# Order and queues of the first transfers: the second half of row block 1, and the first half of Wv in two pieces

## The chip, the core and the metric

The kernel runs on one core of a Trainium2 chip. The core has five engines that run their own instruction streams: TensorE (PE; its weight loads are listed as PEld), VectorE (DVE), ScalarE (ACT), GpSimd (POOL) and SyncE (SP). Transfers between the chip's main memory and the on-chip memory are issued in this kernel from SP and from ACT, each in the order of its own stream, and are carried out by 16 DMA engines that serve both queues (q1 in the profile holds SP's transfers, q10 ACT's). The metric is the device time of one execution in microseconds (us), as the median over runs. The profile is of one further execution; its span runs from the first to the last profiled instruction.

## What is computed

Input x has 2048 rows of 640 values in bf16. It is normalised by rows, and the normalised rows feed two branches: an attention with 32 heads of 20 values, worked in four segments of 512 rows with a running memory between them, and a gated feed-forward branch of width 1536.

```python
xn = _layernorm(x, axis=-1)                       # (x - mean) / sqrt(var + 1e-5)
s = _A_ref(xn, A_wq, A_wk, A_wv, A_wo, A_beta)     # q, k, v = xn @ wq, wk, wv; 4 segments; @ wo
g = _silu(_B_ref(xn, B_w_gate, B_w_up, B_w_down))  # (sigmoid(xn@wg) * (xn@wu)) @ wd
return x + s * g
```

For this change only the beginning matters: x of the first segment and the weights wv, wk, wq come in, the rows are normalised and transposed, and v, then k, then q of the first segment are computed.

## The kernel before

**Tiles.** A segment n is 512 rows, held as four row blocks j of 128 rows (128 partitions) by 640 columns in the tile `xt4` (in the profile `xt`). Each row block has two halves of HD = 320 columns. Weights lie as five chunks (DC = 5) of 128 input rows; `Wv` is 128 partitions x 5 chunks x 640 columns and is loaded in two column halves of 320, `load_wv(0, ...)` and `load_wv(1, ...)` (L149 to L151). A half of `Wv` is 400 KB, a half of a row block 80 KB.

**Order.** The kernel is scheduled by hand: on each engine and queue the instructions run in the order in which the program issues them, and waits between engines come from semaphores that the framework sets by tile and part of a tile. A transfer counts a completion semaphore up to 16. There are eight of these for the transfers of both queues, used in turn, and a transfer waits until the one that last used its semaphore has landed.

**First transfers** (L154 to L164), in program order. On SP: block 0 first half, block 1 first half, block 1 second half, block 2 whole, `Wv` second half, `Wk`, `Wq`, beta. On ACT: block 0 second half, `Wv` first half, block 3 whole; then an activation (L169) that loads the table for square roots, and much later, behind `root0(1)` and `root0(2)`, the weights `Wg` and `Wu`.

**Normalising segment 0** (L648 to L720). For each row block j:

- `half_stats0(j, i)` (L651, VectorE): statistics of half i of the block; it needs that half of x.
- `moments0(j)` (L654, VectorE): mean and variance from the two halves' statistics.
- `root0(j)` (L657, ScalarE): square root of the variance.
- `norm0(j)` (L662, L665, VectorE): reciprocal, then the normalised rows `xn`, for block 0 in two pieces of columns.
- `transpose0(j)` (L675, TensorE): five transposes of 128x128 into `pT`; chunks 0 to 2 are copied into `xnT` by ScalarE (L680), chunks 3 and 4 by VectorE (L678).
- `do_V(0, j, half)` (L344): five matmuls `psv` over the chunks k with `xnT` and `Wv`, evacuated by ScalarE.

On VectorE the order around the change is: statistics of block 0, moments 0, statistics (1, 0), norm 0, statistics (1, 1), moments 1, statistics (2, 0), copy of `xnT` of block 0, norm 1, statistics (2, 1), statistics (3, 0), moments 2, and so on. On TensorE `keep_warm` matmuls into `wps`, whose result nobody uses, stand between the first pieces of real work. After the last `do_V` TensorE goes on with `do_K` and `do_Q` of segment 0 (`psq`, L281), then with gate and up products, attention and the other segments in one fixed order.

Of the kernel before, what the change touches and what calls it, by code (L numbers as in the profile page):

```python
# [9 lines left out]
P = 128  # L10
D = 640
# [6 lines left out]
DC = D // P  # L18
# [4 lines left out]
HD = D // 2  # L23
# [52 lines left out]
def kernel(  # L76
# [14 lines left out]
    nc = tc.nc  # L91
# [36 lines left out]
    def load_x(n, a=0, b=4, cols=slice(0, D), eng=nc.sync):  # L128
        if n not in xt_of:
            xt_of[n] = lnp.tile([P, 4, D], BF, name="xt4", bufs=3)  # L130
        src = x2[n * L:(n + 1) * L, :].rearrange("(j p) d -> p j d", p=P)
        eng.dma_start(xt_of[n][:, a:b, cols], src[:, a:b, cols])
# [6 lines left out]
    Wv = cpool.tile([P, DC, D], BF, name="Wv")  # L139
# [6 lines left out]
    nc.vector.memset(warm[:, 0:L], 0.0)  # L146
    beta_b = cpool.tile([P, H], BF, name="beta_b")

    def load_wv(half, eng):  # L149
        hs = slice(half * HD, (half + 1) * HD)  # L150
        eng.dma_start(Wv[:, :, hs], A_wv[:, hs].rearrange("(c p) n -> p c n", p=P))  # L151


    load_x(0, 0, 1, slice(0, HD))  # L154
    load_x(0, 0, 1, slice(HD, D), nc.scalar)
    load_x(0, 1, 2, slice(0, HD))
    load_wv(0, nc.scalar)
    load_x(0, 1, 2, slice(HD, D))
    load_x(0, 2, 3)
    load_x(0, 3, 4, eng=nc.scalar)  # L160
    load_wv(1, nc.sync)
    load_w(nc.sync, Wk, A_wk)
    load_w(nc.sync, Wq, A_wq)
# [626 lines left out]
    for p in range(0, OLD, 5):  # L790
        n, g = units[p][0], units[p][1][0][0]
# [216 lines left out]
```

## Time and profile before

| what | value |
|---|---|
| median of three timed runs | 317.45 us (317.26 to 317.47) |
| the profiled execution's own time | 317.27 us |
| its span | 315.6 us |
| granted TensorE clock, mean | 1.000 |
| busy, share of the span | PE 98%, PEld 53%, DVE 72%, ACT 72%, POOL 42% |

TensorE is busy almost throughout; VectorE and ScalarE have room on average. That average says little about the first 14 us, in which TensorE waits for rows to be normalised. TensorE's own work there, in order of time (start, length, engine, line, operation, tiles and shape):

```profile
5.20 0.55 PE L675 MATMUL pT<-ident,xn 128*128 128x128 bf16 x5
...
7.44 0.45 PE L675 MATMUL pT<-ident,xn 128*128 128x128 bf16 x5
...
9.35 0.45 PE L675 MATMUL pT<-ident,xn 128*128 128x128 bf16 x5
...
11.13 0.45 PE L675 MATMUL pT<-ident,xn 128*128 128x128 bf16 x5
11.42 2.20 PE L121 MATMUL psv<-Wv,xnT 128*128 128x320 bf16 x15
13.46 5.56 PE L121 MATMUL psq<-xnT,Wk 128*128 128x512 bf16 x25
```

The four rows of `pT` are the transposes of row blocks 0 to 3. [...] The queues' issues in the same view:

```profile
0.79 1.82 SPq L132 DMA_DIRECT2D xt<-in_A_x_dram  x4
2.65 0.43 SPq L151 DMA_DIRECT2D Wv<-in_A_wv_dram  x1
3.25 0.40 SPq L135 DMA_DIRECT2D Wk<-in_A_wk_dram  x1
3.70 0.52 SPq L135 DMA_DIRECT2D Wq<-in_A_wq_dram  x1
5.08 0.81 SPq L164 DMA_DIRECT2D beta_b<-in_A_beta_dram  x1
```

```profile
0.79 0.41 ACTq L132 DMA_DIRECT2D xt<-in_A_x_dram  x1
1.23 0.46 ACTq L151 DMA_DIRECT2D Wv<-in_A_wv_dram  x1
1.72 0.55 ACTq L132 DMA_DIRECT2D xt<-in_A_x_dram  x1
```

The length of such a row is the time in which the transfer is issued, not the time until its data are there. The row of four on SP holds the transfers of L154, L156, L158 and L159.

### The profile page before, as it was taken

To read this page: it belongs to the slowest core of one execution; us is meant where nothing else is said; L and a number is where in the kernel's file an instruction comes from. 1 tells how busy PE (TensorE), PEld (TensorE's weight loads), DVE (VectorE), ACT (ScalarE), POOL (GpSimd) and SP (SyncE) were. 2 spreads that over 40 slices of the span, in tenths; PEclk is the share of its full clock that TensorE was granted. 3 is DMA by queue.
4 is the path that set the end of the run, shared out by engine and by line. 5 is a ranking of instruction groups with operands and counts; after the bars stand their busy time and mean duration, and the time that the engine had idled before them with its cause. 6 is when DMAs were issued, how large, how long until landed. Compare 5 with 4: busy or idle time off the path is not lost.

```text
span 315.6 us, 10266 instructions
## 1 busy us (share of the span) xinstructions
PE 310.3 (98%) x4331; PEld 167.5 (53%) x4331; DVE 225.9 (72%) x512; ACT 227.2 (72%) x231; POOL 131.6 (42%) x227
## 2 busy tenths in 40 slices
PE   8999999999999999999999999999999999999995
PEld 4644445665545445654665454544466655444673
DVE  6473455765868988878869989788787776644575
ACT  3724478778798776778897869679897775777730
POOL 2580035535262534435453364444434353525313
PEclk9999999999999999999999999999999999999999
DMA  7984886420742364405953365139524000280202
GB/s 250 358 338 148 286 223 177 120 50 2 217 147 64 100 144 134 108 23 149 266 169 111 111 111 152 53 112 207 170 88 129 19 23 31 78 157 13 86 23 83
DMA packets 55390, 41.27 MB, mean 131 GB/s; under 512 B 25968, under 2 KB 53968, under 8 KB 55344
## 3 DMA queue, kind: packets, MB, share of 16 engines
q1 hardware_dynamic: 52800, 35.87, 41.1%
q10 hardware_dynamic: 2544, 4.75, 4.1%
q8 instruction: 34, 0.56, 0.8%
q14 instruction: 12, 0.10, 0.1%
HBM read 19.98 MB, written 14.73 MB: 110 GB/s over the span
## 4 chain that ended last, share of the span: by engine, by line
PE 96%; DMA 1%; DVE 1%; SPq 0%; issue 0%
PE up L121 12%; PE yp L121 11%; PE gp L121 11%; PE psq L121 10%; PE Sps L548 8%; PE gp L125 6%; PE yp L125 6%; PE up L125 6%; PE ApsT L572 6%; PE psv L121 5%; PE psq L125 4%; PE sp L121 3%; PE sp L125 3%; PE psv L125 2%; PE sp L532 2%; DMA xt<-in_A_x_dram 1%
## 5 line engine op out<-in xcount | busy, mean ns | idle before, releaser
L556 ACT ACTIVATE pt<-Sps 128x2048 bf16<-128x2048 f32 x80 | 150.3, 1878 | 40.8 <-PE Sps L548 39.5
L558 POOL TENSOR_SCALAR_AFFINE_SELECT pt<-pt 128x512 bf16<-128x512 bf16 x128 | 82.3, 658 | 156.0 <-ACT pt L556 153.2
L435 DVE SCALAR_TENSOR_TENSOR hT<-tg,up 128x512 bf16<-128x512 bf16 x48 | 32.6, 679 | 23.9 <-PE up L121 9.7
L121 PE MATMUL up<-xnT,Wu 128*128 128x512 bf16 x159 | 42.5, 380 | 0.0
L121 PE MATMUL gp<-xnT,Wg 128*128 128x512 bf16 x152 | 40.1, 380 | 0.0
L424 ACT ACTIVATE tg<-gp 128x512 bf16<-128x512 f32 x48 | 28.5, 595 | 14.4 <-PE gp L121 10.5
L121 PE MATMUL yp<-Wd,hT 128*128 128x320 bf16 x246 | 38.2, 300 | 0.0
L548 PE MATMUL Sps<-QT,KT 23*128 23x384 bf16 (+3 forms) x512 | 31.9, 301 | 0.0
L121 PEld LDWEIGHTS <-hT 128*128 128x128 bf16 x246 | 22.7, 98 | 11.3 <-issue 3.0
L580 DVE STREAM_TRANSPOSE tb<-ApsT 128x512 f32<-128x512 f32 x31 | 22.0, 711 | 4.2 <-PE ApsT L572 4.0
L452 DVE SCALAR_TENSOR_TENSOR aa<-t,yp 128x320 bf16<-128x320 bf16 x32 | 15.3, 478 | 13.5 <-ACT t L451 13.4
L125 PE MATMUL gp<-xnT,Wg 128*32 128x512 bf16 x352 | 24.4, 380 | 0.0
L572 PE MATMUL ApsT<-pt,V 128*32 128x512 bf16 (+2 forms) x496 | 23.5, 299 | 0.0
L121 PEld LDWEIGHTS <-Wu 128*128 128x128 bf16 x159 | 14.2, 98 | 17.4 <-issue 4.0
L121 PEld LDWEIGHTS <-Wg 128*128 128x128 bf16 x152 | 14.1, 98 | 15.8 <-issue 1.9
L125 PE MATMUL yp<-Wd,hT 128*32 128x320 bf16 x552 | 21.9, 300 | 0.0
L125 PE MATMUL up<-xnT,Wu 128*32 128x512 bf16 x324 | 21.7, 380 | 0.0
L548 PEld LDWEIGHTS <-KT 23*128 23x128 bf16 x512 | 9.1, 92 | 23.4 <-issue 23.4
L592 DVE STREAM_TRANSPOSE obT<-ob 128x256 f32<-128x256 f32 x31 | 13.5, 434 | 11.1 <-POOL ob L589 11.0
L589 POOL TENSOR_TENSOR ob<-tb,rb 128x320 bf16<-128x320 f32 x27 | 19.9, 736 | 2.3
L121 PE MATMUL psq<-xnT,Wq 128*128 128x512 bf16 x85 | 19.5, 379 | 0.0
L572 PEld LDWEIGHTS <-V 128*32 128x32 bf16 x496 | 14.4, 97 | 8.1 <-ACT tg L424 0.2
(124 smaller groups left out, 448.3 us busy)
## 6 DMA issues: line engine op xcount, KB each, us to landing
KT<-Kd SPq DMA_DIRECT2D x32, 80.0 KB
QT<-Qd SPq DMA_DIRECT2D x32, 80.0 KB
out_dram<-xt SPq DMA_DIRECT2D x14, 160.0 KB
Wg<-in_B_w_gate_dram ACTq DMA_DIRECT2D x1, 1920.0 KB
Wu<-in_B_w_up_dram ACTq DMA_DIRECT2D x1, 1920.0 KB
xt<-in_A_x_dram SPq DMA_DIRECT2D x3, 640.0 KB
Wd<-in_B_w_down_dram SPq DMA_DIRECT2D x1, 1920.0 KB
Od<-odot SPq DMA_DIRECT2D x3, 640.0 KB
```

The source lines that it names most:

```text
L121: nc.tensor.matmul(out_, lhsT=lhsT, rhs=rhs, start=start, stop=stop, skip_group_check=True)
L125: nc.tensor.matmul(out_[cols], lhsT=lhsT[:, cols], rhs=rhs, start=start, stop=stop, tile_position=(0, 32 * r), skip_group_check=True)
L424: nc.scalar.activation(tg[:], gp[:], ACT.Tanh, scale=0.5)
L435: nc.vector.scalar_tensor_tensor(out=h[:], in0=seg[n]["tg"][:], scalar=1.0, in1=up[:], op0=ALU.add, op1=ALU.mult)
L452: nc.vector.scalar_tensor_tensor(out=s["aa"][j][:, hs], in0=t2[:], scalar=1.0, in1=yp[:], op0=ALU.add, op1=ALU.mult)
L548: nc.tensor.matmul(Sps[:, r, c0:c0 + ncol], lhsT=KT[32 * r:32 * r + DH + 3, g, kb * P:(kb + 1) * P], rhs=QT[32 * r:32 * r + DH + 3, g, q0: ...
L556: nc.scalar.activation(pt[:, :, 0:ntot], Sps[:, :, 0:ntot], ACT.Exp, scale=SCALE)
L558: nc.gpsimd.affine_select(out=pt[:, :, c0:c0 + P], in_=pt[:, :, c0:c0 + P], compare_op=ALU.is_ge, fill=0.0, base=0, pattern=[[0, 4], [1, P ...
L572: nc.tensor.matmul(ps[32 * r:32 * r + 32, q0:L], lhsT=Vflat[n % 2][:, off:off + 32], rhs=t[:, r, c0:c0 + ncol], start=(i == 0), stop=(i == ...
L580: nc.vector.transpose(tb[:].rearrange("p h e -> p (h e)"), ps[:].rearrange("p (a t b) -> p a b t", t=32, b=2))
L589: eng.tensor_tensor(to, of, by, op=ALU.mult)
L592: nc.vector.transpose(s["obT", g // 4][:, g % 4, :].bitcast(F32), ob[:].rearrange("p a e b -> p (a e b)").bitcast(F32))
```

## The change

The second half of row block 1 moves from SP's queue to ACT's and stands there ahead of `Wv`, as the second transfer. The first half of `Wv`, one transfer on ACT before, becomes two: chunks 0 to 2 on ACT, chunks 3 and 4 on SP, where they take the place that the second half of block 1 had. All else stays as it was. SP's issues ahead of `Wk` stay five in number; ACT's ahead of the table load go from three to four.

```diff
-    def load_wv(half, eng):
+    def load_wv(half, eng, c0=0, c1=DC):
         hs = slice(half * HD, (half + 1) * HD)
-        eng.dma_start(Wv[:, :, hs], A_wv[:, hs].rearrange("(c p) n -> p c n", p=P))
+        eng.dma_start(Wv[:, c0:c1, hs], A_wv[c0 * P:c1 * P, hs].rearrange("(c p) n -> p c n", p=P))
 
 
     load_x(0, 0, 1, slice(0, HD))
     load_x(0, 0, 1, slice(HD, D), nc.scalar)
     load_x(0, 1, 2, slice(0, HD))
-    load_wv(0, nc.scalar)
-    load_x(0, 1, 2, slice(HD, D))
+    load_x(0, 1, 2, slice(HD, D), nc.scalar)
+    load_wv(0, nc.scalar, 0, 3)
+    load_wv(0, nc.sync, 3, DC)
     load_x(0, 2, 3)
     load_x(0, 3, 4, eng=nc.scalar)
     load_wv(1, nc.sync)
```

## The prediction

> **What bounds the kernel now.** I began with the page's chain of work that ended last. By engine it is
>
> ```profile
> PE 96%; DMA 1%; DVE 1%; SPq 0%; issue 0%
> ```
>
> TensorE holds the whole span except for a small share of DMA and VectorE. The change touches only the first transfers, so the next view is that chain in order of time, over its first 60 us (start, length, what):
>
> ```profile
> 1.66 0.05 issue
> 1.71 3.82 DMA xt<-in_A_x_dram
> 5.53 0.02 issue
> 5.55 0.50 DVE st L651
> ...
> 6.29 0.36 DVE st L651
> 6.64 0.20 DVE xnT L678
> ...
> 6.89 0.45 PE psv L121 x2
> ...
> 13.62 10.79 PE psq L121 x50
> ```
>
> One transfer of x, issued at 1.71 us on SP, lands at 5.53. It is the second half of row block 1 (L158), and VectorE's statistics of that half, half_stats0(1, 1), wait for it. VectorE's stages then hand on to TensorE, and from there the chain is TensorE's alone. The timeline of VectorE and ScalarE shows how long the waiting is:
>
> ```profile
> 2.29 1.28 ACT L169 ACT_TABLE_LOAD   x1 [2.29 <-issue]
> 4.24 0.29 ACT L657 ACTIVATE rs<-mv,epsc 128x1 f32<-128x1 f32 x1 [0.45 <-DVE mv L654]
> 4.76 0.64 DVE L665 TENSOR_SCALAR xn<-xt,mv,rs 128x384 bf16<-128x384 bf16 x2
> 5.55 0.49 DVE L651 BATCH_NORM_STATS2 st<-xt 128x6 f32<-128x320 bf16 x1
> 6.08 0.21 DVE L654 BATCH_NORM_AGGREGATE mv<-st 128x2 f32<-128x12 f32 x1
> 6.20 0.44 DVE L651 BATCH_NORM_STATS2 st<-xt 128x6 f32<-128x320 bf16 x1
> ```
>
> The reader is to see that VectorE is free at 4.76 + 0.64 = 5.40 and starts again at 5.55, while the statistics at 6.20 (block 2, first half) start before the instruction ahead of them has ended at 6.29. The third view, TensorE's waits between 2 and 14 us, and between 14 and 300 us, says who uses what VectorE makes (total, times, longest):
>
> ```profile
> PEld L675 <- DVE xn L665: 1.2, 4, 0.3
> PEld L121 <- DVE xnT L678: 0.5, 1, 0.5
> ```
>
> ```profile
> PEld L125 <- DVE odot L413: 0.5, 2, 0.2
> PEld L572 <- ACT tg L424: 0.2, 1, 0.2
> ```
>
> At the start all four blocks' transposes wait for VectorE's normalised rows. Later, besides its own issue gaps, TensorE waits for others 0.7 us in all. So a VectorE stage that comes t earlier throughout the start brings all later TensorE work t earlier; nothing after 14 us swallows it.
>
> **Landings.** From the counts of the semaphores in the trace (a transfer has landed at the 16th), in us: block 0 3.05 (SP) and 3.23 (ACT), block 1 first half 3.70, first half of Wv 5.07, block 1 second half 5.53, block 3 5.70, block 2 6.10, second half of Wv 7.29. The two queues took turns by whole transfers: SP, ACT, SP, ACT and so on. The DMA view of 3 to 4 us agrees, with ACT's queue (q10, the Wv half) moving nearly everything while SP's (q1) block 1 half, issued at 1.71, stood:
>
> ```profile
> q10 hardware_dynamic: 408, 0.26, 94.0%
> q1 hardware_dynamic: 35, 0.02, 5.4%
> ```
>
> **The change part by part.**
>
> *Second half of block 1 from SP to ACT, ahead of Wv.* It is issued on ACT at about 1.23 instead of on SP at 1.71, and only 82 kB each of three other transfers stand before it instead of those and 410 kB of Wv. Its nearest row is the block's first half, issued at 1.24 and landed at 3.70; behind that by one turn (82 kB at the 225 GB/s of 2 to 3 us, 0.36) it lands near 4.1, over 1 us before VectorE wants it. The statistics then start as a released one does, 0.08 before the predecessor's end (6.20 against 6.29; 7.30 against 6.94 + 0.45): 5.40 - 0.08 = 5.32 instead of 5.55, a gain of 0.23. The wait removed is replaced by VectorE's own work. Shifted by 0.23 come the moments (5.84), the statistics of block 2 (5.97), the copy of xnT (6.33), norm0(1) (ended 7.16), so TensorE's transposes of block 1 at 7.21 instead of 7.44, and with the same steps those of block 3 at 10.90 instead of 11.13. ScalarE's root0(1) follows the moments at 6.09, when its copy of xnT (5.57 to 6.05) has ended.
>
> *Block 2 is what could be late next.* It must be there by 5.97 and landed at 6.10. It is still the fourth transfer on SP, issued at about 2.18. With turns by transfers the order becomes blocks 0 and 1, two Wv pieces, block 2, block 3: it and block 3 change places, so I take block 3's old landing, 5.70, and a cost of 0. The other end is 6.10: statistics at 6.12, which costs 0.15.
>
> *Two Wv pieces, on ACT (chunks 0 to 2) and SP (3, 4).* The bytes ahead of their end are those that had landed at 5.53 before; the first product needs them when ScalarE's copy ends at 6.06, and the fourth matmul waits for VectorE's copy until 6.61 anyway. Margin about 0.5, cost 0. Beyond it each 0.1 us of lateness costs up to 0.1. SP's count of issues before the second half of Wv stays at four. [...]
>
> *One issue more on ACT.* ScalarE's table load waits behind the issues in program order. Starts of issues lie 0.44 to 0.49 apart and the third took 0.55; the fourth moves the load from 2.29 to between 2.74 and 2.87, its end to between 4.02 and 4.15, and the small activation behind it (0.20 long) ends between 4.24 and 4.37. Behind that stands root0(0), which began at 4.24 and which norm0(0) waits for. ScalarE too starts an instruction up to 0.10 before the last ends (10.10 against 9.72 + 0.48). Ends: 0 and 0.13. I take 0.02, because most issues took the shorter time. Wg and Wu are issued at 6.33 and 8.33 behind root0(1) and root0(2), and come earlier with them; those queues hold more than a microsecond of bytes, so nothing depends on it.
>
> *Completion counters.* Eight are used in turn: Wk, the ninth transfer, was issued at 3.25 only when a half of block 0 had landed. Now the second half of Wv is the ninth. It goes from 2.65 to 3.25 on SP, Wk to 3.70, Wq and beta each about 0.45 later. First packets come about 1.03 after the issue (0.79 to 1.82), so Wv's second half is ready at 4.3 and its turn comes after 5.4: hidden, with 1.1 to spare. It is wanted at 7.73 - 0.23 = 7.50 and landed at 7.29, a margin of 0.2. Wk landed at 9.52 and is wanted at 13.2.
>
> **Sum.** -0.23 + 0 + 0 + 0.02 + 0 = -0.21 us. The profiled execution took 317.27 us (span 315.6, 1.7 around it that the change leaves alone), so 317.06. The median of the runs shown is 317.45, 0.18 above it; 317.45 - 0.21 = 317.24, and I forecast 317.2. Ends of the unknown terms: -0.23 to +0.05.
>
> **Rivals.**
>
> *Shares by packets.* If the queues share evenly in small turns rather than transfer by transfer, blocks 2 and 3 end together with the last bytes, at 6.10. The statistics of block 2 then start at 6.12, and of 0.23 only 0.08 is left: 317.4. Against it stand the 94% and 5% above; for it, that between 4 and 5 us both queues moved packets. [...]
>
> *It doesn't do what it says.* The half is still not there at 5.32, because the pieces of Wv pass it. It stands ahead of them on its own queue, and only 246 kB are before it, so I give this little; the time stays at 317.45. ScalarE's late table load, at its far end, leaves 317.35 and looks much the same.
>
> *Slower: block 2 takes block 1's place.* VectorE's order is fixed, so with block 2 later than 6.19 everything behind stands. The windows show 225 GB/s in 2 to 3 us, 277 in 3 to 4, 373 in 4 to 5:
>
> ```profile
> 2.00:3.00 1.00, 1.00 (x28) 0.73 (x24) 0.00 (x0) 0.71 (x1) 0.27 (x3) 1.00 0.96 225
> 3.00:4.00 1.00, 1.00 (x28) 0.73 (x23) 0.89 (x3) 0.78 (x2) 0.00 (x0) 1.00 0.99 277
> 4.00:5.00 1.00, 1.00 (x21) 0.55 (x13) 0.96 (x4) 0.29 (x1) 0.00 (x0) 1.00 1.12 373
> ```
>
> If more small rows on both queues keep it at 225, the 902 kB up to block 2 need 4.0 us from 1.9, and its landing some 0.55 after the last packet (5.55 to 6.10 before) is 6.45: +0.27, 317.7. With block 3 ahead of it as well, 1,066 kB, it lands at 7.2: +1.0, 318.45. Against it: the low rate is that of the first packets, and 3 to 4 us was Wv almost alone.
>
> **Chances.** Forecast 0.47; shares by packets 0.12; nothing gained 0.11; block 2 late 0.15, half of it over 318.1; 0.15 for what one profile can't show, such as a start that meets later transfers in another phase, of which 0.11 go to much faster and 0.04 to much slower. A measurement of this kernel tells 0.2%, 0.63 us, from no change; nothing in the sum reaches that, so no change within it holds 0.77, faster 0.11, slower 0.12. Alone the forecast lies between 317.0 and 317.5. The range runs from 316.7 to 318.0: up into the late block 2, and down 0.3 below the lowest run less the gain (317.26 - 0.23), a little over the spread of the runs shown (0.21).
>
> **What would show it.** The changed profile should have half_stats0(1, 1) at 5.32 with no wait, block 2's statistics at 5.97, the transposes of block 3 near 10.90, the first product of Wk near 13.23 instead of 13.46, the table load near 2.75 and root0(0) still at 4.24. I am wrong if VectorE waits for block 2, if root0(0) starts after 4.3, if TensorE waits for Wv near 6 or 7.5, or if the 0.2 us gained by 14 us is gone before the end.

## The result, and the profile after

Over 20 runs each the changed kernel took 318.19 us in the median (317.64 to 320.21), the kernel before 317.51 (317.26 to 318.1): a ratio of 1.0022, 95% interval 1.0015 to 1.0030. The forecast was 317.2 and its range ended at 318.0, so the time lies above both. The profiled execution took 318.22 us with a span of 316.5, against 317.27 and 315.6 before.

The page's chain by engine still reads as TensorE's, with one share doubled:

```profile
PE 96%; DMA 2%; DVE 1%; ACTq 0%; issue 0%
```

In order of time, the first 36 us of the chain of the changed kernel (start, length, what):

```profile
1.24 0.45 ACTq L132
1.69 0.03 issue
1.72 5.27 DMA Wv<-in_A_wv_dram
6.99 0.04 issue
7.03 0.99 PE psv L121 x5
...
8.57 0.02 issue
8.60 1.52 PE psv L121 x10
...
14.38 10.79 PE psq L121 x50
```

Where block 1's second half stood (issued 1.71, landed 5.53) there is now the first piece of Wv: issued 1.72, landed 6.99. TensorE's first product of Wv starts at 7.03 instead of 6.11. The product at 8.60 waits for Wv's second half too. K's first rows appear at 14.38 instead of 13.62, and nothing later gives that 0.76 back.

VectorE and ScalarE of the changed kernel in the timeline (start, length, then the instruction, idle time before it in brackets):

```profile
5.33 0.49 DVE L652 BATCH_NORM_STATS2 st<-xt 128x6 f32<-128x320 bf16 x1
5.85 0.21 DVE L655 BATCH_NORM_AGGREGATE mv<-st 128x2 f32<-128x12 f32 x1
6.83 0.49 DVE L652 BATCH_NORM_STATS2 st<-xt 128x6 f32<-128x320 bf16 x1 [0.78 <-DMA xt<-in_A_x_dram]
...
7.62 0.45 DVE L666 TENSOR_SCALAR xn<-xt,mv,rs 128x640 bf16<-128x640 bf16 x1
```

```profile
2.76 1.28 ACT L170 ACT_TABLE_LOAD   x1 [2.76 <-issue]
4.06 0.20 ACT L170 ACTIVATE epsc<-epsc 128x1 f32<-128x1 f32 x1
4.25 0.29 ACT L658 ACTIVATE rs<-mv,epsc 128x1 f32<-128x1 f32 x1
```

The wait that the change removes is gone: block 1's second half is read at 5.33. But the next statistics, of block 2, wait 0.78 us for a transfer that landed at 6.81, and block 1's norm starts at 7.62 instead of 6.94. On ScalarE the table load moved from 2.29 to 2.76, and root0(0) stayed where it was (4.25).

Both late landings begin in one stretch. First the DMA view of 3 to 4 us of the kernel before, in 40 slices of 25 ns, and then the same of the changed kernel:

```profile
GB/s 154 77 102 102 179 205 256 282 230 256 307 256 256 205 256 205 230 230 256 205 230 256 282 282 282 333 333 410 358 384 384 333 333 333 384 358 384 384 384 384
```

```profile
DMA  9999755591222300802493329914394438443995
GB/s 359 358 308 308 205 154 179 154 128 51 52 51 51 51 0 26 77 26 77 154 128 102 102 77 77 102 51 154 77 154 154 154 102 154 128 154 102 154 205 154
```

After 3.2 us the DMA engines of the changed kernel move little (the first line is the share of time that their packets took, in tenths). From the start of the span until 4.5 us 528 kB had been moved, against 694 kB before; the gap was 195 kB at 5.0 and 242 kB at 7.0. The windows of the changed kernel say the same (the last column is GB/s; before, 277 and 373):

```profile
3.00:4.00 1.00, 1.00 (x28) 0.72 (x24) 0.89 (x2) 1.00 (x1) 0.00 (x0) 1.00 0.61 131
4.00:5.00 1.00, 1.00 (x21) 0.54 (x13) 0.95 (x4) 0.53 (x3) 0.00 (x0) 1.00 1.02 284
```

Between 3 and 4 us the rate fell to less than half (277 to 131), the share of time that packets took (the last column but one) only from 0.99 to 0.61. So the engines were not simply idle; some packets took longer too. And both queues moved at once, which the DMA view of this stretch shows by packets:

```profile
q1 hardware_dynamic: 105, 0.06, 37.9%
q10 hardware_dynamic: 121, 0.07, 23.1%
```

### The profile page after: what moved, and what is told of

The parts are those of the page before. It is cut to its first block, busy times and chain, and to the rows that moved or that the text cites. A ratio compares the mean times of both kernels' runs of the same rounds, so it can differ in the third digit from the quotient of the medians.

```text
span 316.5 us, 10262 instructions
## 1 busy us (share of the span) xinstructions
PE 311.0 (98%) x4331; PEld 168.0 (53%) x4331; DVE 226.0 (71%) x512; ACT 227.0 (72%) x231; POOL 131.9 (42%) x227
## 4 chain that ended last, share of the span: by engine, by line
PE 96%; DMA 2%; DVE 1%; ACTq 0%; issue 0%
PE up L121 11%; PE yp L121 11%; PE gp L121 11%; PE psq L121 10%; PE Sps L549 8%; PE gp L125 6%; PE yp L125 6%; PE up L125 6%; PE ApsT L573 5%; PE psv L121 5%; PE psq L125 4%; PE sp L121 3%; PE sp L125 3%; PE psv L125 2%; DMA Wv<-in_A_wv_dram 2%; PE sp L533 2%
## 5 line engine op out<-in xcount | busy, mean ns | idle before, releaser
L121 PE MATMUL psv<-Wv,xnT 128*128 128x320 bf16 x115 | 18.4, 299 | 0.4 <-DMA Wv<-in_A_wv_dram 0.4
```

Source lines behind the costliest of these rows:

```text
L121: nc.tensor.matmul(out_, lhsT=lhsT, rhs=rhs, start=start, stop=stop, skip_group_check=True)
```

## The experiments

Four theories stood at the start or came on the way. **A**: two pieces of Wv, fed from two queues at once, are slow. **B**: Wv is issued 0.5 us later than before (1.72 instead of 1.23), and the short transfers ahead of it are used up before its packets come. **C**: block 1's half on ACT starves the queues whenever Wv is issued. **D**, which the expectation of h1 names: every transfer issued near 1.7 us is slow, whatever it carries. A rate under 200 GB/s between 3 and 4 us is called the dip.

All runs, with what their profiles show: when the first (or only) piece of Wv's first half was issued, the rate between 3 and 4 us, when block 2 and all of that half had landed (all 16 counts of the transfer's semaphore), and the median with its ratio to the kernel before on the same chip.

| run | Wv issued | GB/s, 3 to 4 us | block 2 | Wv | median us | ratio (95%) |
|---|---|---|---|---|---|---|
| before | 1.23 | 277 | 6.10 | 5.07 | 317.51 | |
| changed | 1.72 | 131 | 6.81 | 6.99 | 318.19 | 1.0022 (1.0015 to 1.0030) |
| r1 changed, again | 1.72 | 163 | 6.37 | 6.50 | 317.78, one run | |
| e1 Wv in one piece | 1.72 | 172 | 6.06 | 8.21 | 318.57 | 1.0041 (1.0016 to 1.0066) |
| e2 split alone | 1.23 | 297 | 6.12 | 6.18 | 317.60 | 1.0004 (0.9996 to 1.0013) |
| e3 block 1 whole | 1.24 | 287 | 5.76 | 5.86 | 317.36 | 1.0005 (0.9993 to 1.0018) |
| g1 delay alone | 1.72 | 133 | 6.11 | 6.79 | 318.46 | 1.0031 (1.0020 to 1.0043) |
| g2 first piece early | 1.23 | 315 | 5.86 | 5.40 | 317.65 | 1.0015 (1.0005 to 1.0024) |
| g3 block 2 ahead | 1.72 | 181 | 5.67 | 6.80 | 318.32 | 1.0030 (1.0017 to 1.0044) |
| g4 as e3 | 1.24 | 289 | 5.70 | 5.80 | 317.17 | 0.9994 (0.9985 to 1.0003) |
| h1 all x first | 2.20 | 178 | 6.20 | 8.69 | 320.49 | 1.0100 (1.0085 to 1.0115) |
| h2 e3 with a delay | 1.72 | 176 | 5.93 | 7.92 | 318.26 | 1.0025 (1.0007 to 1.0043) |
| h3 as e3 | 1.23 | 298 | 5.67 | 5.69 | 317.24 | 1.0002 (0.9988 to 1.0017) |
| h4 e3, Wv split | 1.23 | 296 | 5.99 | 7.09 | 317.85 | 1.0011 (1.0002 to 1.0020) |
| i1 e3, four on ACT | 1.23 | 311 | 5.75 | 5.15 | 317.37 | 0.9995 (0.9986 to 1.0004) |
| i2 e3, split, three on ACT | 1.24 | 293 | 5.41 | 6.30 | 317.32 | 0.9994 (0.9986 to 1.0003) |
| i3 late, whole, three on ACT | 1.72 | 152 | 6.51 | 7.89 | 318.21 | 1.0024 (1.0005 to 1.0042) |

**r1.** The changed kernel, unaltered.

> The changed kernel once more, unaltered, for a second profile. Theory A (the two pieces of Wv, issued at the same moment on both queues, are fed slowly) and theory B (Wv is issued 0.5 us later than before, and the short transfers ahead of it are used up before its packets come) both expect the same again: under 200 GB/s between 3.0 and 4.0 us, block 2 landed between 6.4 and 7.1 us, the first piece of Wv last at 6.5 to 7.2. If the dip is an accident of one execution, the rate there is over 280 and block 2 lands before 6.2.

It came again, somewhat milder: block 2 at 6.37, Wv at 6.50. The dip is no accident; its length varies from run to run.

**e1, one piece.** The split undone, the move kept.

```diff
-    load_wv(0, nc.scalar, 0, 3)
-    load_wv(0, nc.sync, 3, DC)
+    load_wv(0, nc.scalar)
```

> Both halves of block 1 second as in the change, but the first half of Wv in one transfer, on ACT behind its half of block 1; block 2 is then third on SP. Theory A: Wv runs at full rate once it begins, as before the change (over 300 GB/s from 3.5 us on), block 2 lands near 4.5, Wv before 6.0, and VectorE's gain of 0.2 us is kept: 317.3, ratio 0.999. Theory B: Wv is issued at 1.72 here too, so the queues still run low between 3.3 and 4 us (under 250 GB/s), Wv lands after 6.3 and TensorE's first product waits for it: 317.8 to 318.2.

Worse than either theory said. The dip came without any split, and theory A's main claim fell. The chain shows what TensorE waited for:

```profile
1.72 6.49 DMA Wv<-in_A_wv_dram
8.21 0.04 issue
8.25 0.84 PE psv L121 x5
```

**e2, split alone.** Order and queues of the kernel before, Wv's first half in two transfers on ACT.

```diff
-    load_wv(0, nc.scalar)
+    load_wv(0, nc.scalar, 0, 3)
+    load_wv(0, nc.scalar, 3, DC)
```

> The order of the kernel before, with the first half of Wv in two transfers, both on ACT, one behind the other; block 1's second half stays on SP. Theory A in its wide form (a transfer cut in two is dearer by itself) expects a dip after 3 us and block 1's second half later than 5.8, 317.8 or more. Theory B, and theory A in its narrow form (two queues at once), expect the times of before: first half of Wv landed near 5.1, block 1's second half near 5.5 or earlier, since its turn can now come between the pieces, and 317.3 to 317.5.

No dip, and a time that can't be told from before. Block 1's second half landed at 5.29, between the pieces, and VectorE's wait was gone; block 2 at 6.12 then held VectorE instead.

**e3, block 1 whole.** Block 1 early, and Wv not late: one transfer in place of the two halves, so Wv keeps its second place on ACT.

```diff
-    load_x(0, 1, 2, slice(0, HD))
-    load_x(0, 1, 2, slice(HD, D), nc.scalar)
-    load_wv(0, nc.scalar, 0, 3)
-    load_wv(0, nc.sync, 3, DC)
+    load_x(0, 1, 2)
+    load_wv(0, nc.scalar)
     load_x(0, 2, 3)
```

> Block 1 whole in one transfer, second on SP; the first half of Wv whole and second on ACT as before the change, issued at 1.23; block 2 third on SP. Both theories expect no dip, since Wv is neither split nor late: block 1 lands near 4.1, Wv near 5.4, block 2 before 5.97, VectorE starts the statistics of block 1's second half at 5.32, and the 0.23 us of the prediction are kept: 317.2 to 317.3, ratio 0.9993. If neither holds and moving block 1's half forward is by itself what starves the queues, block 2 lands after 6.2 and the time is 317.6 or more.

The landings came close to what was expected: 4.07, 5.86 and 5.76, and no dip. VectorE ran through, as its timeline shows:

```profile
5.35 0.48 DVE L650 BATCH_NORM_STATS2 st<-xt 128x6 f32<-128x320 bf16 x1
5.87 0.21 DVE L653 BATCH_NORM_AGGREGATE mv<-st 128x2 f32<-128x12 f32 x1
5.99 0.44 DVE L650 BATCH_NORM_STATS2 st<-xt 128x6 f32<-128x320 bf16 x1
```

In this profile nothing came of it: block 3's transposes stood at 11.13 as before. In the chain TensorE alone led from 1.24 us on, and its transposes were 106 ns apart up to about 7 us, where the kernel before had 55.

**g1, delay alone.** Before's order; 4 kB ahead of Wv on ACT, which cost Wv one issue slot (issued at 1.72 instead of 1.23).

```diff
+    load_x(0, 3, 4, slice(0, 16), nc.scalar)
     load_wv(0, nc.scalar)
...
-    load_x(0, 3, 4, eng=nc.scalar)
+    load_x(0, 3, 4, slice(16, D), nc.scalar)
```

> The order of the kernel before, but a transfer of block 3's first 16 columns (4 kB) stands on ACT between block 0's half and the first half of Wv, which stays one transfer; block 1's second half stays on SP. Wv is thus issued at about 1.72 instead of 1.23 and nothing else of weight moves. Theory B (Wv's issue is late and the short transfers ahead of it are used up) expects the dip of the changed kernel: under 200 GB/s between 3 and 4 us, Wv landed after 6, 317.8 or more. Theory C (putting block 1's half on ACT is what starves the queues, whenever Wv is issued) expects the rates of before, over 270, and 317.4 to 317.6.

The dip came (133 GB/s) with block 1's half on SP, and theory C fell. The tiny transfer has rows of 32 bytes, which marks the place in ACT's packets: they ended by 3.1 us, the first packet of Wv came after 3.2, 1.5 us after its issue, and the queue passed 30 packets a 0.1 us only near 4.0. Its time is not clean, because the rest of block 3 waited for a semaphore and pushed ScalarE's table load to 3.62. h2 repeats the test without that.

**g2, first piece early.** On ACT the three chunks of Wv ahead of block 1's half, the rest as in the change.

```diff
-    load_x(0, 1, 2, slice(HD, D), nc.scalar)
     load_wv(0, nc.scalar, 0, 3)
+    load_x(0, 1, 2, slice(HD, D), nc.scalar)
     load_wv(0, nc.sync, 3, DC)
```

> The changed kernel with two lines exchanged on ACT: the three chunks of Wv are issued second (1.23), block 1's second half third, behind them; the other two chunks stay on SP third. Theory B expects no dip (over 270 GB/s between 3 and 4 us), block 1's second half landed near 4.7, Wv before 5.8, block 2 before 6.2, and 317.2 to 317.6. Theory C, and theory A as far as it still stands (pieces on both queues), expect a dip under 200 and 317.8 or more.

Exchanging two lines of the change removes the dip (315 GB/s) with both queues still carrying pieces. Wv and block 2 landed as theory B had it (5.40, 5.86), block 1's second half at 5.42 instead of 4.7, so VectorE still waited 0.15 us for it. The time was a little over the band, and its interval lies above 1: without the dip the pieces still gain nothing.

**g3, block 2 ahead.** Block 2 ahead of the piece of Wv on SP.

```diff
-    load_wv(0, nc.sync, 3, DC)
     load_x(0, 2, 3)
+    load_wv(0, nc.sync, 3, DC)
```

> The changed kernel with block 2 ahead of Wv's chunks 3 and 4 on SP; ACT as in the change. Which of the two late landings costs the time? If it is block 2 alone, VectorE no longer waits, block 2 lands near 4.5 and the time falls to 317.3. If Wv is as late as block 2 (theory B, 1.72 on ACT and 2.18 on SP), TensorE's first product of Wv starts after 6.8 all the same and the time stays at 317.7 to 318.3.

Block 2 came in time for VectorE (5.67, read at 5.96), and the time did not fall: TensorE's first product of Wv started at 6.84. So Wv's lateness is enough by itself; in the changed kernel block 2 and Wv are late side by side.

**g4.** The kernel of e3 again.

> Block 1 whole on SP once more, for a second profile and more times. In its first profile TensorE ran at half its rate until about 7 us (transposes 106 ns apart, 55 in the kernel before) and the chain was TensorE's own from 1.24 us on. If that ate the 0.23 us that VectorE gained, a profile in which the transposes of block 0 are 55 ns apart shows block 3's transposes near 10.9 and a span near 315.3; one with 106 ns shows 11.13 and 315.55 again. Times: 317.2 to 317.4 in most runs.

This time the transposes of block 0 stood 56 ns apart, and the gain of the prediction appeared. The chain of g4:

```profile
10.97 0.43 PE pT L674 x5
...
13.43 0.22 PE psq L121
```

Block 3's transposes start at 10.94, K at 13.27, and the span is 315.3.

**h1, all x first.** All of x ahead of Wv, which is issued at 2.20.

```diff
-    load_wv(0, nc.scalar, 0, 3)
-    load_wv(0, nc.sync, 3, DC)
     load_x(0, 2, 3)
     load_x(0, 3, 4, eng=nc.scalar)
+    load_wv(0, nc.scalar)
     load_wv(1, nc.sync)
```

> All row blocks of segment 0 ahead of Wv: blocks 0 and 1 in halves on both queues as in the change, then block 2 on SP and block 3 on ACT (issued near 1.72), and the whole first half of Wv fourth on ACT (2.2). Theory B (what counts is when Wv is issued, and how much short work stands ahead of it): block 2 and 3 land before 5.2, VectorE never waits, Wv lands near 6.5 to 7.5 and TensorE waits for it: 318.0 to 319. If instead every transfer issued near 1.7 is slow, whatever it carries, blocks 2 and 3 land after 5.5 too.

Later issue, later landing, but two parts of the expectation missed. Blocks 2 and 3 landed late as well (6.20, 6.39; the ninth of their 16 counts, called the middle one below, at 4.80 and 4.97). That is the outcome of D, and against B as it was put. And the time was far over it, because TensorE came back from its wait at half rate:

```profile
8.73 1.49 PE L121 MATMUL psv<-Wv,xnT 128*128 128x320 bf16 x5 [2.69 <-DMA Wv<-in_A_wv_dram]
10.02 0.42 PE L635 MATMUL wps<-mn 128*128 128x256 bf16 x1
10.23 0.74 PE L675 MATMUL pT<-ident,xn 128*128 128x128 bf16 x5
```

Five transposes take 0.74 here and 0.45 in the profile before. The windows of h1 show it in the granted clock (the third last column, 1.00 is full rate):

```profile
6.00:7.00 1.00, 0.04 (x1) 0.10 (x1) 0.78 (x4) 0.33 (x2) 0.00 (x0) 1.00 1.09 345
7.00:8.00 1.00, 0.00 (x0) 0.00 (x0) 0.98 (x3) 0.00 (x0) 0.00 (x0) 0.67 0.95 317
8.00:9.00 1.00, 0.27 (x2) 0.15 (x2) 0.37 (x2) 0.00 (x0) 0.00 (x0) 0.50 1.06 387
...
13.00:14.00 1.00, 1.00 (x8) 0.69 (x7) 0.00 (x0) 0.33 (x1) 0.00 (x0) 0.50 1.03 392
14.00:15.00 1.00, 1.00 (x11) 0.77 (x10) 0.38 (x2) 0.78 (x3) 0.00 (x0) 0.92 1.03 386
```

TensorE went idle at 6.04, the clock was halved at 7.34 and came back at 14.17. That is a second price of a late Wv. Two profiles show it (h1, its longest run, and h2), and the mean clocks say that it is behind most of the longest runs of the late kernels: 13 runs of all the study have a mean granted clock of 0.995 or less, all 13 are of kernels with Wv issued at 1.72 or later (the changed kernel's 320.21 is one, all five of h1 are), and they took 319.84 to 321.89. One run of i3 took as long, 320.08, at 0.999, so there is another cause too.

**h2, e3 with a delay.** The clean form of g1.

```diff
     load_x(0, 1, 2)
+    load_x(0, 3, 4, slice(0, 16), nc.scalar)
     load_wv(0, nc.scalar)
     load_x(0, 2, 3)
-    load_x(0, 3, 4, eng=nc.scalar)
+    load_x(0, 3, 4, slice(16, D), nc.scalar)
```

> Block 1 whole on SP, the order that showed no dip, with one thing added: 4 kB of block 3 (16 columns) in a transfer of their own on ACT ahead of the first half of Wv, which is so issued at 1.72 instead of 1.23. Block 1's half is not on ACT, Wv is in one piece, and the bytes ahead are the same. Theory B expects the dip back (under 220 GB/s between 3 and 4 us), Wv landed 0.5 us or more later than in the kernel without the delay (5.8), and TensorE waiting for it: 317.6 to 318.4. If the issue time were harmless: 317.2 to 317.4.

Against h3 on the same chip, 4 kB ahead of Wv cost 318.26 - 317.24 = 1.0 us: the rate fell to 176, Wv landed at 7.92. Nothing else of weight was changed, so Wv's place behind one more transfer is enough. The size is rough: the runs of each spread over 2.5 us (317.26 to 320.46, and 317.06 to 319.55). Three of its 11 runs (319.84 to 320.46) have a mean clock of 0.995; the profiled one (320.12) is among them, and its clock was halved for 3.41 us. The median is not of those.

**h3.** The kernel of e3 a third time.

> Block 1 whole on SP a third time, beside the two above on one chip, for the interval of the one version that may beat the kernel before. With TensorE at full rate from 5.2 us on the gain is 0.2 to 0.25 us, with half rate until 7 us none, so 317.1 to 317.4 and a ratio of 0.9990 to 1.0000.

317.24 against 317.54, with some runs up to 319.55 that spoil the interval. The transposes of block 0 were 106 ns apart here, yet block 3's stood at 10.96: full rate was there by 6.4 us, not only at 7 as in e3. What counts is how long the half rate lasts.

**h4, e3 with Wv split on ACT.**

```diff
-    load_wv(0, nc.scalar)
+    load_wv(0, nc.scalar, 0, 3)
+    load_wv(0, nc.scalar, 3, DC)
```

> Block 1 whole on SP, and the first half of Wv in two transfers, both on ACT, the first issued at 1.23. In the version with Wv in one piece most runs took 317.1 to 317.3, but 7 of 36 took 318 to 319.6. If those are runs in which the last engine's share of Wv lands after TensorE wants it (5.7 to 5.9 in three profiles, wanted near 6.1 to 6.4), the first three chunks alone now land near 4.6 and the other two are wanted 0.4 later, so the slow ones disappear: median 317.2, none over 318. If they have another cause, such as block 2's last share, about one run in five stays over 318.

The expectation failed. The slow runs did not go, the whole got slower, and the second piece's last share landed at 7.09 though its middle one had landed at 5.30.

**i1, i2, i3.** Three versions to take the split, the fourth transfer on ACT and the late issue apart. i1 is e3 with block 3 in two halves on ACT; i2 is h4 with block 3 on SP; i3 is e1 with block 3 on SP.

```diff
 i1
-    load_x(0, 3, 4, eng=nc.scalar)
+    load_x(0, 3, 4, slice(0, HD), nc.scalar)
+    load_x(0, 3, 4, slice(HD, D), nc.scalar)
 i2, i3
-    load_x(0, 3, 4, eng=nc.scalar)
+    load_x(0, 3, 4)
```

> Block 1 whole on SP, Wv's first half whole and second on ACT (1.23), and block 3 in two halves, so that ACT issues four transfers. If the fourth transfer on ACT is what lowers the rate after 4 us, it is 330 or less in 4 to 6 us, tails grow and the time is 317.6 or more. If the split of Wv does it, the rates are 355 and more and the time is 317.2 to 317.4, as with three transfers.

> Block 1 whole on SP, Wv's first half in two transfers on ACT (1.23 and 1.72), block 3 fourth on SP, so that ACT issues three transfers only. If the split of Wv lowers the rate after 4 us, it is 330 or less and the last share of Wv's second piece lands after 6.2: 317.6 or more. If it is the fourth transfer on ACT, the rates are 355 and more: 317.2 to 317.4.

> Both halves of block 1 second on the two queues as in the change, Wv's first half in one piece third on ACT (1.72), block 3 fourth on SP: late issue without a split and without a fourth transfer on ACT. The dip between 3 and 4 us comes (under 200 GB/s). If the late issue is the whole of it, the rate is back over 340 from 4.5 us on and Wv lands near 6.0 to 6.5, 317.5 to 318; if its long tail belongs to the late issue too, Wv lands after 6.8, 318 or more.

The number of transfers on ACT does not lower the rate: i1 has 371 GB/s between 4 and 5 us. The split does, to 321 in i2; but there Wv's second piece at 6.30 still came in time, and the time stayed at 317.32 where 317.6 was expected. h4 differs from i2 only in block 3, on ACT instead of SP, and took 317.85; why is not shown. i3 has neither, only the late issue: the dip is there, the long tail is there (Wv's middle count 5.79, its last 7.89), and so are 318.21 us.

Over all profiles the line is sharp. The 8 with Wv issued at 1.72 or later, the changed kernel's two among them, show 131 to 181 GB/s between 3 and 4 us, and the 9 with 1.23 or 1.24 show 277 to 315, whichever queue, split or order of blocks they have. The split shows one microsecond later: of the 9 early ones, the four with Wv whole after block 1 and the kernel before have 358 to 373 GB/s between 4 and 5 us, and the four with Wv in pieces (e2, g2, h4, i2) 277 to 321.

Two things the line leaves open. In all 8 late kernels at least one more transfer of x stands between block 0's half and Wv on ACT, so the runs don't part the time of Wv's issue from its place in the queue. For the time speaks that by count of ACT's packets Wv's first one comes 1.4 to 1.8 us after its issue in every kernel, early or late, but h1 (2.0). And theory B is right only in part: the queues were not empty. In e1, g3 and h1, which have block 2 third on SP, issued at 1.71, 74 to 78 of its 128 packets (the first of 1,280 bytes on SP's queue) had started by 4.0 us, the first at about 3 us and the last only after 5.2. What was issued near 1.7 us came, but slowly, as D has it; in the early kernels Wv, issued at 1.23, filled that stretch.

## Why the prediction failed

*The step that failed* is the pricing of the two landings by bytes. Of Wv: "The bytes ahead of their end are those that had landed at 5.53 before", margin 0.5, cost 0. Of block 2: "it and block 3 change places, so I take block 3's old landing, 5.70, and a cost of 0." Both take it that the DMA engines move what has been issued at a steady rate, one whole transfer after the other. Neither held: the rate fell to 131, and both queues moved side by side. The working priced the later issue of Wv's second half, of Wk and of Wq, and never that of Wv's first half, which went from 1.23 to 1.72 behind block 1's half. It stood in the open: the timeline of the kernel before has the issues 0.49 apart. The four short transfers ahead, 328 kB, were moved by about 3.2 us, where before 410 kB of Wv, issued at 1.23, had just begun to flow; with the first packet 1.5 us after the issue (g1) and a slow start after that, an issue at 1.72 leaves a hole that none of the other orders tried filled (e1, g3, h1, i3).

*Term by term.* The gain: statistics of block 1's second half at 5.33 (5.32 forecast), its landing at 3.65 (4.1): right. Block 2: cost 0 with an end at 0.15; it landed at 6.81 and block 1's transposes went from 7.44 to 8.12, a loss of 0.68 in place of a gain of 0.23 (Wv's late product kept TensorE until then as well). The two pieces of Wv: margin 0.5; they landed at 6.12 and 6.99, and were 0.9 late. The second half of Wv: forecast to be hidden with a margin of 0.2 at its landing; it landed at 8.56 and TensorE waited for it. The issue on ACT: 0.02; root0(0) did not move, but 0.11 us go with it elsewhere (last section). Completion counters: the second half of Wv issued at 3.23 (3.25): right. That nothing after 14 us would swallow a shift: right, with the other sign; of the 0.94 us in the span 0.76 stand at the first scores already.

*The rivals.* "Block 2 takes block 1's place" has the wait that came and a range, 317.7 to 318.45, that holds the time, at a chance of 0.15. The number is partly luck: with block 2 in time the loss stays (g3). Nor was its reason right: small rows on both queues don't keep the rate at 225 (e3 and i1 mix them and have 358 and 371 between 4 and 5 us). Shares by packets: the queues did move side by side between 3 and 4 us, but its 317.4 took the rate to stay, and it fell. "It doesn't do what it says": no, it does, and the half is there 1.7 us early.

What stays open is why what is issued near 1.7 us moves so slowly until about 4 us, why the first packets of Wv take 1.4 to 1.8 us from their issue (2.0 in h1) where block 0's take 1.03 on SP and 1.18 on ACT (the kernel before), and why the last shares lag so far after a late start. That lag may be why the loss differs from run to run (317.64 to 318.78 for 19 runs of the changed kernel; the 20th, 320.21, has a mean clock of 0.995). Nor is it shown why an issue slot cost more than its own length: one of 0.49 us ahead of Wv cost 1.0 us (h2 against h3).

**A better version.** Block 1 whole on SP and Wv whole and second on ACT keeps what the change wanted: medians of 317.36, 317.17 and 317.24 against 317.47, 317.44 and 317.54, though no interval excludes 1, and 7 of its 36 runs took 318.0 or more. i1, the same with block 3 in halves, had none of those in 11 runs (317.24 to 317.78) at 317.37 against 317.64, and i2 none either (317.07 to 317.83) at 317.32. All are within what a measurement of this kernel tells from no change.

## What to carry to other kernels

The bytes ahead of a transfer were not enough here to price its landing at the start of a kernel: they gave 5.53 for the two pieces of Wv's first half, and the last landed at 6.99. Write down for every transfer when it is issued, when its first packet can come, and what moves until then; here it paid to issue the large load second, not third (317.24 in h3, 318.26 in h2). The transfer moved forward on ACT's queue pushed the issue of those behind it by a slot (Wv from 1.23 to 1.72, block 3 from 1.72 to 2.20), and the one that hurt was the large one. Where two small pieces were wanted early, one transfer that held both cost one slot less than two (Wv issued at 1.24 in e3, at 1.72 in the changed kernel).

## What the runs showed of the hardware

**TensorE's half rate.** It shows in two ways. At the start of the kernel transposes at 5.2 us stood 55 or 56 ns apart in seven of the profiles and 106 or 107 in others, with the same fillers ahead of them. The views print a granted clock of 1.00 for both, but the trace's own records of the clock begin only where full rate does: at 4.89 us in the kernel before, 6.26 in h3, 6.59 in the changed kernel, 7.00 in e3. It explains how e3 could gain VectorE's 0.23 us and show none of it. It does not explain the loss in the changed kernel's profile: full rate was there before Wv was (6.59 against 6.99). Later the granted clock does fall: by the same records in h1 from 7.34 to 14.17, in h2 from 7.78 to 11.19. These stretches last 6.83 and 3.41 us. When the clock fell in h1, TensorE had been idle for 1.3 us (6.04 to 7.34), and busy for 1.77 of the 3.41 us from the start of full rate up to the fall. In e1 a wait of 1.82 us from 6.4 on cost no clock in the profiled run, with TensorE busy for only 1.50 of its first 3.41 us at full rate, and two other runs of e1 have a mean clock of 0.995 (320.08 and 320.23). So neither the idle time (1.82 us against 1.3) nor the busy time (1.50 against 1.77) tells whether the clock falls; what does is not shown.

**With a fourth issue on ACT one activation comes later, 150 us on.** The same exponential of ScalarE, before and in the changed kernel:

```profile
156.29 1.88 ACT L556 ACTIVATE pt<-Sps 128x2048 bf16<-128x2048 f32 x1 [0.25 <-POOL pt L558]
```

```profile
157.33 1.88 ACT L557 ACTIVATE pt<-Sps 128x2048 bf16<-128x2048 f32 x1 [0.53 <-POOL pt L559]
```

Its releaser came at the same place relative to the work around it; it started 0.27 us after it, and TensorE's next scores 0.11 us later. All 11 profiles of kernels with four transfers on ACT show these 0.11 us, and none of the other six. Why is not known.
